# A linear-attention and GELU kernel: one activation table, unit loads of 112 rows, a mask and a copy taken bank by bank, and range checks put later

## The chip, the cores and the metric

The kernel runs on one core of one Trainium2 chip. The metric is the device time of one execution in microseconds. Before the change it was 520.96 us, the median of three runs (520.43 to 521.4).

## The reference

A gated linear attention is followed by a feed-forward block with an exact GELU, all in float32.

```python
# q, k, v, alpha: (4, 8, 768, 48); alpha drawn between 0.8 and 1.0
for t in range(S):
    state = alpha[:, :, t, :, None] * state + np.einsum('bhd,bhe->bhde', k[:, :, t], v[:, :, t])
    y[:, :, t] = np.einsum('bhd,bhde->bhe', q[:, :, t], state)
x = y.transpose(0, 2, 1, 3).reshape(3072, 384)
h = x @ w_in                                   # 384 x 2048
g = 0.5 * h * (1.0 + erf(h * inv_sqrt2))
return g @ w_out                               # 2048 x 384
```

## The kernel before

The 3072 tokens are cut into 12 groups of 256 tokens, and each group into two units of four heads, so there are 24 units, numbered 0 to 23. The text writes u0, u1 and so on. A unit goes through these steps:

- **load** (SP, some of the first on ACT's queue): alpha, k and q of the unit into the tiles `ad`, `kd`, `qd` (L165 for units 0 to 3, L168 for the others), and v into `vn` once a group (L170). There are two sets of these tiles, so the load of unit n overwrites what unit n-4 read.
- **scan, times, back, keys** (DVE): a running product of alpha into `pp` (L254) with its two small helpers into `pe` and `rp` (L255, L256), q times it (L259), a running product from the other end into `rp` (L263), k times that (L268).
- **scores** (PE): q against k (L283), and the transposed k (L291), both into one pair of PSUM banks: in each bank the first half holds scores and the second half transposed keys. `sbank` is that pair, `sfirst` an extra one for u1.
- **kn** (ACT, L301) copies the transposed keys out, **mask** (DVE, L306) multiplies the scores by a causal mask into `ss`. Both read both banks of the pair.
- **inside** (PE): scores against v (L323) and keys against v (L340) into `ybank` or `yfirst`. **chain** (DVE, L358, L360) adds up the states, **outer** (PE, L384) multiplies q by them, **carry** (DVE, L365) keeps the last state.
- **xh, xl** (ACT L435, DVE L439): the result split into a rounded part and its rest, in the tile `x`; the last heads go to `z` and are spread into `x` by six small transfers once a group (`spread`, L448, three on SP and three on ACT's queue in the first groups).
- **check** (ACT, L176): two activations per unit that sum how far alpha lies outside its range, into `junk`. Nothing of the normal path reads it before the end; but the load of unit n waits for the checks of unit n-4.

The feed-forward weights come in 16 pieces of 768 KB (`fetch`, L203, three staging buffers `st`), w_in and w_out in turn. A piece is converted into a high and a low part by four steps: ACT copies its top words (L218), DVE joins them (L222), ACT rounds (L232, `wih` or `woh`), DVE subtracts (L235, `wil` or `wol`). The last step frees the staging buffer. Two pieces make one f of eight. The text writes f0 to f7.

A group's feed-forward is eight times gemm1 (PE, L456, 18 matmuls into `hp`), two GELU activations (ACT, L522 and L523), a subtraction (DVE, L528, `glo`) and gemm2 (PE, L540, 12 matmuls into `acc`). Groups 0 to 3 run so, each f as soon as its weights are there; from group 4 on two groups are taken together (`wide1`, `wide2`, L472 and L490).

The order of each engine's instructions is written out by a planner at the end of the kernel: every step is an `Op` with an engine, a guessed cost, a list of steps that it waits for, and a rank. The planner plays them forward in time and emits them in the order of their planned starts. The engines then run these orders strictly, and wait for each other by semaphores. A guess of a cost sets an order and nothing else.

The lines of the change are `load_data`, `turned_out`, `masked`, `plan_unit` and the loop that plans the units.

Of the kernel before, what the change touches and what calls it, by code (L numbers as in the profile page):

```python
# [16 lines left out]
ALU = mybir.AluOpType  # L17
# [20 lines left out]
def gla_then_gelu_ffn(ctx: ExitStack, tc: tile.TileContext, q, k, v, alpha, qg, kg, ag, vg, q0, k0, a0, w_in, w_out, out):  # L38
# [61 lines left out]
    def small_bank(shape, name):  # L100
        t = sbank
        n = 1
        for d in shape[1:]:
            n *= d
        t = t[:, 0, :n]
        return t if len(shape) == 2 else t.rearrange("p (a b) -> p a b", a=shape[1])

    warm = small_bank([P, P], "warm")
# [50 lines left out]
    def load_data(g, u):  # L159
        n, p = NU * g + u, slice(2 * u, 2 * u + 2)  # L160
        for i, (name, first, src) in enumerate((("a", a0, ag), ("k", k0, kg), ("q", q0, qg))):
            to = data[g % NB][name][:, p].rearrange("p a t -> p (a t)")
            if n < NB * NU:
                eng = nc.scalar if n < NU and (i + u) % 2 else nc.sync
                eng.dma_start(to, first[n])  # L165
                continue
            for h in range(2):
                nc.sync.dma_start(to[h * DP : h * DP + D], src[g - NB, u, h])  # L168
        if u == NU - 1:
            nc.sync.dma_start(vbuf[g % NB][:, :, : HV * D], vg[g])  # L170
# [524 lines left out]
    def op(*args, **kw):  # L695
        ops.append(Op(*args, **kw))
        return ops[-1]
# [4 lines left out]
    def plan_unit(n):  # L702
# [12 lines left out]
        d["load"] = op("SP", "load", lambda: load_data(g, u), [old.get(x) for x in ("outer", "scores", "inside", "c0", "c1")], rank=r - 30, lands=2.0, kb=786 if old == {} else 590)  # L715
        d["load"].cost = 0.9 if n < NU else 1.4 if old == {} else 2.6
# [52 lines left out]
    for n in range(n_units):  # L769
        plan_unit(n)  # L770

# [175 lines left out]
def _laid_out(q, k, v, alpha, moe_w_in, moe_w_out):  # L947
# [14 lines left out]
    def spare(x, value):  # L962
        x = x[:2].reshape(4, 2, D, 512)
        return _np.concatenate((x, _np.full((4, 2, 64 - D, 512), value, x.dtype)), axis=2).reshape(4, P, 512)

    qg, kg, ag = grouped(q), grouped(k), grouped(alpha)
    kg = kg.reshape(-1, H // 4, 2, D, 2, 4, 64).swapaxes(4, 5).reshape(ag.shape)
# [6 lines left out]
        "qg": qg[2:],  # L974
        "kg": kg[2:],
        "ag": ag[2:],
# [3 lines left out]
        "q0": spare(qg, 0.0),  # L980
        "k0": spare(kg, 0.0),
        "a0": spare(ag, 1.0),
# [36 lines left out]
```

## Time and profile before

| what | value |
| --- | --- |
| median of three runs | 520.96 us |
| the profiled execution | 520.84 us |
| its span, first to last instruction | 519.0 us |
| around the span | 1.84 us |
| PE busy (matmuls) | 489.8 us, 94% of the span |
| DVE busy | 251.8 us, 49% |
| ACT busy | 200.4 us, 39% |
| mean granted TensorE clock | 0.972 of 2.4 GHz |

The times in the rows are microseconds from the start of the span. PE is the matmul engine, PEld its weight loads, SPq and ACTq the transfers that SP and ACT issue. In a timeline the first column is the start, the second the length, and a bracket says how long the engine had idled before and what it waited for. On one engine instructions overlap by some tens of ns, so the distance from one start to the next is what an instruction takes from the engine.

### The profile page before, as it was taken

Reading aid. Unit: us, or ns where it says so; the run is one execution under the profiler, and the core shown is the slowest. Engines: PE = TensorE matmul, PEld = TensorE weight load, DVE = VectorE, ACT = ScalarE, POOL = GpSimd, SP = SyncE. Lnnn points to the kernel's source line nnn. Section 1 sums busy time; section 2 is a strip of 40 time slices with the busy share of each in tenths; the row PEclk is TensorE's granted clock in tenths of the full one; section 3 lists DMA queues with packets and bytes.
Section 4 is the critical chain, followed back from the end, with each engine's and each line's share of the span. In section 5 each row is a group of like instructions: output and inputs, shape, how many; then the busy total and the mean of one; then the engine's idle time right before and its main releaser. Section 6 shows DMA issues by size and latency. Waiting matters only on the chain.

```text
span 519.0 us, 12171 instructions
## 1 busy us (share of the span) xinstructions
PE 489.8 (94%) x5190; PEld 418.8 (81%) x5190; DVE 251.8 (49%) x486; ACT 200.4 (39%) x386; POOL 31.3 (6%) x42
## 2 busy tenths in 40 slices
PE   5657999999999999999999999999999999999994
PEld 5556889899998999988888777788777788888883
DVE  4879977998888565121111558521433121211212
ACT  1647757445543342222222543232544222231311
POOL 2000001112211111000000101100000000000000
PEclk9569999999999999999999999999999999999998
DMA  8587757325541421000000332300100000100001
GB/s 317 176 268 230 239 145 231 92 58 159 139 129 43 140 80 46 1 30 1 1 1 1 107 92 56 85 1 0 63 18 3 14 1 0 62 0 1 0 1 67
DMA packets 24542, 40.20 MB, mean 77 GB/s; under 512 B 3872, under 2 KB 11616, under 8 KB 24480
## 3 DMA queue, kind: packets, MB, share of 16 engines
q1 hardware_dynamic: 22736, 34.06, 22.0%
q0 software_dynamic: 880, 3.93, 2.0%
q10 hardware_dynamic: 864, 1.34, 0.8%
q8 instruction: 43, 0.70, 0.6%
q14 instruction: 19, 0.16, 0.1%
HBM read 32.24 MB, written 4.72 MB: 71 GB/s over the span
## 4 chain that ended last, share of the span: by engine, by line
PE 82%; DVE 7%; ACT 4%; DMA 4%; issue 1%; SPq 0%; ACTq 0%; DVEq 0%
PE hw L472 26%; PE accw L490 17%; PE acc L540 10%; PE hp L456 9%; PE ybank L490 8%; DMA st<-in_moe_w_in_dram 2%; PE sbank L283 2%; PE sbank L291 2%; PE sbank L323 1%; PE sbank L384 1%; DMA ad<-in_ag_dram 1%; DVE st L222 1%; DVE pp L254 1%; ACT top L218 1%; PE ybank L323 1%
## 5 line engine op out<-in xcount | busy, mean ns | idle before, releaser
L528 DVE TENSOR_TENSOR glo<-hw,ghi 128x512 fp32r<-128x512 f32 x64 | 44.2, 691 | 172.3 <-ACT hw L523 172.3
L472 PE MATMUL hw<-x,wih 128*128 128x512 f32 x384 | 121.9, 398 | 0.0
L522 ACT ACTIVATE ghi<-hw 128x512 fp32r<-128x512 f32 x64 | 38.3, 598 | 177.7 <-PE hw L472 177.7
L472 PEld LDWEIGHTS hw<-x,wih 128*128 128x128 f32 x384 | 71.0, 188 | 16.1
L456 PE MATMUL hp<-x,wih 128*128 128x256 f32 x384 | 73.5, 291 | 7.6 <-DMA x<-z 7.5
L472 PE MATMUL hw<-x,wil 128*128 128x512 f32 x192 | 75.9, 395 | 0.0
L456 PEld LDWEIGHTS hp<-x,wih 128*128 128x128 f32 x384 | 60.9, 194 | 9.0 <-ACT top L218 7.7
L456 PE MATMUL hp<-x,wil 128*128 128x256 f32 x192 | 54.8, 286 | 0.0
L490 PE MATMUL accw<-ghi,woh 128*128 128x512 f32 x128 | 51.1, 399 | 0.0
L490 PE MATMUL accw<-ghi,wol 128*128 128x512 f32 x128 | 50.2, 393 | 0.0
L540 PE MATMUL acc<-woh,ghi 128*128 128x384 f32 x128 | 44.9, 351 | 0.0
L472 PEld LDWEIGHTS hw<-x,wil 128*128 128x128 f32 x192 | 36.0, 188 | 9.0
L540 PE MATMUL acc<-wol,ghi 128*128 128x384 f32 x128 | 43.0, 336 | 0.0
L490 PE MATMUL accw<-glo,woh 128*128 128x512 f32 x128 | 40.3, 391 | 0.0
L522 ACT ACTIVATE ghi<-hp 128x512 fp32r<-128x512 f32 x32 | 19.1, 598 | 52.3 <-PE hp L456 51.3
L523 ACT ACTIVATE hw<-hw 128x512 f32<-128x512 f32 x64 | 37.9, 592 | 0.0
L456 PEld LDWEIGHTS hp<-x,wil 128*128 128x128 f32 x192 | 37.3, 194 | 0.0
L263 DVE TENSOR_TENSOR_SCAN rp<-ad,rp,top 128x255 f32<-128x255 f32 x48 | 36.8, 809 | 0.1
L259 POOL TENSOR_TENSOR qd<-qd,pp 128x512 f32<-128x512 f32 x18 | 23.5, 1308 | 200.6 <-DMA st<-in_moe_w_in_dram 81.6
L528 DVE TENSOR_TENSOR glo<-hp,ghi 128x512 fp32r<-128x512 f32 x32 | 22.0, 686 | 22.3 <-ACT hp L523 22.1
L254 DVE TENSOR_TENSOR_SCAN pp<-ad,top 128x256 f32<-128x256 f32 x48 | 30.4, 675 | 4.9 <-DMA ad<-in_a_dram 4.9
L306 DVE TENSOR_TENSOR ss<-sbank,mask 128x512 f32<-128x512 f32 x23 | 15.9, 690 | 29.3 <-ACT kn L301 29.1
(105 smaller groups left out, 695.3 us busy)
## 6 DMA issues: line engine op xcount, KB each, us to landing
st<-in_moe_w_in_dram SPq DMA_DIRECT2D x8, 768.0 KB, 5.8
st<-in_moe_w_out_dram SPq DMA_DIRECT2D x8, 768.0 KB, 5.8
vn<-in_vg_dram SPq DMA_DIRECT2D x12, 384.0 KB, 5.1
ad<-in_ag_dram SPq DMA_DIRECT2D x40, 96.0 KB, 3.0
kd<-in_kg_dram SPq DMA_DIRECT2D x40, 96.0 KB, 2.3
qd<-in_qg_dram SPq DMA_DIRECT2D x40, 96.0 KB, 2.7
out_dram<-parts POOLq DMA_DIRECT2D x3, 768.0 KB, 3.6
x<-z SPq DMA_DIRECT2D x63, 32.0 KB, 2.0
```

Of the source, the lines that this page charges most:

```text
L254: nc.vector.tensor_tensor_scan(pp[:, i], at[:, i], top, MID, ALU.mult, ALU.min)
L259: (nc.vector if g < NSB else nc.gpsimd).tensor_tensor(out=qt, in0=qt, in1=pp, op=ALU.mult)
L263: nc.vector.tensor_tensor_scan(rp[:, i, G - 2 :: -1], at[:, i, G - 1 : 0 : -1], top[:, 1:], rp[:, i, G - 1 :], ALU.mult, ALU.min)
L283: nc.tensor.matmul(d["s"][o, h, t], lhsT=d["kt"][r, (2 * j + i) * CS : (2 * j + i + 1) * CS], rhs=d["qt"][r, i, t], start=True, stop=True)
L306: nc.vector.tensor_tensor(out=d["ss"], in0=d["s"][:, :, : 2 * C].rearrange("p h (c t) -> p h c t", t=CS), in1=mask.unsqueeze(1).unsqueeze( ...
L456: nc.tensor.matmul(hp[:, j, :], lhsT=a[:, j, i * P : (i + 1) * P], rhs=x[:, i, :], start=(i == 0 and n == 0), stop=(i == NK - 1 and n == 2),)
L472: nc.tensor.matmul(h, lhsT=a[:, j, i * P : (i + 1) * P], rhs=x[:, i, part], start=(i == 0 and n == 0), stop=(i == NK - 1 and n == 2),)
L490: nc.tensor.matmul(acc[i], lhsT=w[:, j, e], rhs=a, start=(f == 0 and k == 0 and w is wo_hi[f2]), stop=(f == NF - 1 and k == 1),)
L522: nc.scalar.activation(ghi, hp, AF.Gelu)
L523: nc.scalar.activation(hp, hp, AF.Gelu)
L528: nc.vector.tensor_tensor(out=glo, in0=hp, in1=ghi.bitcast(F32), op=ALU.subtract)
L540: nc.tensor.matmul(acc[t], lhsT=a[:, j, t * C : (t + 1) * C], rhs=w[:, j, :], start=(first and j == 0 and k == 0 and w is wo_hi[f]), stop= ...
```

## The change

The kernel is changed in six places:

- `nc.scalar.preload_act_table(AF.Gelu)` stands ahead of everything that ACT does.
- All units are loaded by three transfers. Units 0 to 3 still bring 128 rows; the others bring 112 rows in one transfer instead of twice 48. The host array holds 16 filler rows between the two halves of 48.
- The copy of k of units 0 and 1 is two instructions, the second bank first; their mask is two instructions, the first bank first.
- In the plan, the checks of groups 0 and 1 wait for the first `spread`.
- In the plan, the first step of the first two weight pieces waits for the copies of k of units 0 and 1.
- The planner's guesses for loads and for `spread` are changed.

```diff
-            if n < NB * NU:
-                eng = nc.scalar if n < NU and (i + u) % 2 else nc.sync
-                eng.dma_start(to, first[n])
-                continue
-            for h in range(2):
-                nc.sync.dma_start(to[h * DP : h * DP + D], src[g - NB, u, h])
+            rows = slice(0, P if n < NB * NU else DP + D)
+            eng = nc.scalar if n < NU and (i + u) % 2 else nc.sync
+            eng.dma_start(data[g % NB][name][rows, p].rearrange("p a t -> p (a t)"), src[n, rows])
...
-        nc.scalar.copy(d["kn"], d["s"][:, :, 2 * C : 4 * C])
+        for b in (slice(1, 2), slice(0, 1)) if NU * g + u < NU else (slice(0, 2),):
+            nc.scalar.copy(d["kn"][:, b], d["s"][:, b, 2 * C : 4 * C])
...
-        nc.vector.tensor_tensor(
-            out=d["ss"],
-            in0=d["s"][:, :, : 2 * C].rearrange("p h (c t) -> p h c t", t=CS),
-            in1=mask.unsqueeze(1).unsqueeze(1).to_broadcast([P, 2, NCH, CS]),
-            op=ALU.mult,
-        )
+        for b in (slice(0, 1), slice(1, 2)) if NU * g + u < NU else (slice(0, 2),):
+            nc.vector.tensor_tensor(
+                out=d["ss"][:, b],
+                in0=d["s"][:, b, : 2 * C].rearrange("p h (c t) -> p h c t", t=CS),
+                in1=mask.unsqueeze(1).unsqueeze(1).to_broadcast([P, b.stop - b.start, NCH, CS]),
+                op=ALU.mult,
+            )
...
-        d["load"].cost = 0.9 if n < NU else 1.4 if old == {} else 2.6
+        d["load"].cost = 0.9 if n < NU else 1.4
...
             d["c%d" % side] = op("ACT", "check", lambda side=side: range_check(g, u, side), [d["xh"]], rank=200 + n)
+            if g == 1:
+                for o in (unit[u]["c%d" % side], d["c%d" % side]):
+                    o.deps.append(ready_x[0])
         if u == NU - 1:
             ready_x[g] = op("SP", "spread", lambda: spread(g), [d["xl"]], rank=-100, lands=3.2)
-            if g >= NSB:
-                ready_x[g].cost *= 2
+            ready_x[g].cost *= 2 if g >= NSB else 0.8
...
     for n in range(n_units):
         plan_unit(n)
+    for n in range(NU):
+        wops[n]["u"].deps.append(unit[n]["kn"])
```

What the planner makes of it is seen at three places. In the rows below a transfer is `DMA tile<-array`, and numbers behind names only tell buffers apart.

The first is ACT's queue at the start of the program. `kn` is the copy of k, `top` the first step of a weight piece, `sbank` and `sfirst` the scores of u0 and u1. Before:

```order
L165 DMA kd_111<-in_k_dram 128x512
L165 DMA ad_110<-in_a_dram 128x512
L165 DMA qd_112<-in_q_dram 128x512
L218 ACT_TABLE_LOAD
L218 CAST top_168<-st_182 128x768
L301 COPY kn_0_235<-sbank 128x512
L218 CAST top_169<-st_184 128x768
L301 COPY kn_1_312<-sfirst 128x512
```

And now:

```order
L108 ACT_TABLE_LOAD
L165 DMA kd_112<-in_kg_dram 128x512
L165 DMA ad_111<-in_ag_dram 128x512
L165 DMA qd_113<-in_qg_dram 128x512
L299 COPY kn_0_235<-sbank 128x256 x2
L215 CAST top_169<-st_183 128x768
L299 COPY kn_1_314<-sfirst 128x256 x2
L215 CAST top_170<-st_185 128x768
```

The table load has gone ahead of ACT's transfers, and each copy of k ahead of the weight piece that it stood behind. The table load ahead of the first GELU, further down the queue, is gone.

The second is SP's queue around the first `spread`. `st` are weight pieces, `x<-z` is the spread of group 0, and `ad`, `kd`, `qd` behind it is the load of u4. Before:

```order
L170 DMA vn_113<-in_vg_dram 128x4x192
L203 DMA st_380<-in_moe_w_out_dram 128x2x1536
L168 DMA ad_110<-in_ag_dram 48x512 x2
L168 DMA kd_111<-in_kg_dram 48x512 x2
L168 DMA qd_112<-in_qg_dram 48x512 x2
L448 DMA x_351<-z_382 16x512 x3
L203 DMA st_414<-in_moe_w_in_dram 128x2x1536
L203 DMA st_418<-in_moe_w_out_dram 128x2x1536
```

And now:

```order
L167 DMA vn_114<-in_vg_dram 128x4x192
L200 DMA st_384<-in_moe_w_out_dram 128x2x1536
L447 DMA x_360<-z_386 16x512 x3
L200 DMA st_403<-in_moe_w_in_dram 128x2x1536
L200 DMA st_409<-in_moe_w_out_dram 128x2x1536
L200 DMA st_477<-in_moe_w_in_dram 128x2x1536
L165 DMA ad_111<-in_ag_dram 112x512
L165 DMA kd_112<-in_kg_dram 112x512
L165 DMA qd_113<-in_qg_dram 112x512
```

The load of u4 has gone from ahead of the spread to behind three more weight pieces.

The third is the end of gemm1 of f3 (`hp_3`), on PE and on DVE. `ybank<-qd,state` is outer of u3, `sbank<-qd,kd` and `sbank<-ident,kd` the scores of u4, `acc` gemm2. On PE before:

```order
L456 MATMUL hp_3_720<-x_351,wil_144 128x256
L384 MATMUL ybank<-qd_116,state_0_124 48x64 x4
L384 MATMUL ybank<-qd_116,state_1_125 48x64 x4
L384 MATMUL ybank<-qd_116,state_2_126 48x64 x4
L384 MATMUL ybank<-qd_116,state_3_127 48x64 x4
L540 MATMUL acc_0_0_559<-woh_151,ghi 128x384
```

And on PE now:

```order
L455 MATMUL hp_3_739<-x_360,wil_145 128x256
L383 MATMUL ybank<-qd_117,state_0_125 48x64 x4
L383 MATMUL ybank<-qd_117,state_1_126 48x64 x4
L383 MATMUL ybank<-qd_117,state_2_127 48x64 x4
L383 MATMUL ybank<-qd_117,state_3_128 48x64 x4
L280 MATMUL sbank<-qd_113,kd_112 64x64 x16
L288 MATMUL sbank<-ident,kd_112 128x128 x4
L539 MATMUL acc_0_0_549<-woh_153,ghi 128x384
```

On DVE now, at the same place, `state_1` to `state_4` being the chain of u3 and `kd_112` the keys of u4:

```order
L219 SCALAR_TENSOR_TENSOR st_594<-st_594,top_169 128x768
L232 TENSOR_TENSOR wol_161<-st_588,woh_153 128x768
L256 TENSOR_TENSOR qd_113<-qd_113,pp_0_645 128x512
L232 TENSOR_TENSOR wil_146<-st_594,wih_138 128x768
L359 TENSOR_TENSOR state_1_126<-ybank,state_0_125 128x96
L359 TENSOR_TENSOR state_2_127<-ybank,state_1_126 128x96
L359 TENSOR_TENSOR state_3_128<-ybank,state_2_127 128x96
L359 TENSOR_TENSOR state_4_129<-ybank,state_3_128 128x96
L260 SCALAR_TENSOR_TENSOR rp_0_646<-ad_111,rp_0_646,top 128x255 x2
L265 TENSOR_TENSOR kd_112<-kd_112,rp_0_646 128x2x4x64
```

The scores of u4 now stand directly behind outer of u3, where gemm2 stood, and both wait for DVE steps that stand behind four conversion steps and a product.

## Rows read from the trace of the kernel before

**Rows 1.** The page's span in 40 equal slices of 13 us: busy tenths of PE, and the granted TensorE clock in tenths.

```profile
PE   5657999999999999999999999999999999999994
PEclk9569999999999999999999999999999999999998
```

**Rows 2.** Busy time by stretches: the stretch and its length, busy us of each engine with its instructions, the granted clock, the share of the DMA engines in use, GB/s.

```profile
7.70:12.30 4.60, 1.32 (x37) 0.98 (x36) 3.52 (x8) 1.51 (x2) 0.00 (x0) 1.00 1.04 404
12.40:31.90 19.50, 7.81 (x212) 6.62 (x212) 16.12 (x32) 11.22 (x20) 0.00 (x0) 0.50 0.62 204
31.90:36.10 4.20, 4.14 (x22) 3.94 (x22) 4.06 (x8) 0.93 (x1) 0.00 (x0) 0.50 0.74 254
44.00:57.00 13.00, 10.62 (x184) 9.37 (x182) 12.50 (x27) 9.32 (x14) 0.00 (x0) 1.00 0.61 189
```

**Rows 3.** The longest of PE's waits over the whole span: the line, what it waited for, us in total, times, the longest.

```profile
PE hp L456 <- DMA x<-z: 7.5, 1, 7.5
```

**Rows 4.** Timeline of the start: ACT, DVE and PE around the mask of u0, and the mask and inside of u1.

```profile
9.83 0.66 PE L291 MATMUL sbank<-ident,kd 128*128 128x128 f32 x4
10.65 0.67 DVE L259 TENSOR_TENSOR qd<-qd,pp 128x512 f32<-128x512 f32 x1
10.77 1.28 ACT L218 ACT_TABLE_LOAD   x1 [10.77 <-DMA st<-in_moe_w_in_dram]
12.98 0.57 ACT L301 COPY kn<-sbank 128x512 f32<-128x512 f32 x1
13.66 0.69 DVE L306 TENSOR_TENSOR ss<-sbank,mask 128x512 f32<-128x512 f32 x1 [2.33 <-ACT kn L301]
19.26 0.69 DVE L306 TENSOR_TENSOR ss<-sfirst,mask 128x512 f32<-128x512 f32 x1 [0.82 <-ACT kn L301]
20.01 1.13 PE L323 MATMUL yfirst<-ss,vn 64*64 64x64 f32 x32 [0.58 <-DVE ss L306]
22.37 0.25 DVE L358 COPY state<-yfirst 128x96 f32<-128x96 f32 x1
```

**Rows 5.** Steps on 128x256 values, half the size of a copy or a mask, and the spread: timeline of ACT, DVE, SP's and ACT's queues and PE.

```profile
24.84 0.35 ACT L435 CAST z<-yfirst 128x256 fp32r<-128x256 f32 x1
25.09 0.37 ACT L435 CAST x<-yfirst 128x256 fp32r<-128x256 f32 x1
25.49 0.42 DVE L439 TENSOR_TENSOR z<-yfirst,z 128x256 fp32r<-128x256 f32 x1
25.83 0.42 DVE L439 TENSOR_TENSOR x<-yfirst,x 128x256 fp32r<-128x256 f32 x1
29.49 2.07 SPq L448 DMA_DIRECT2D x<-z  x3
31.96 0.77 PE L456 MATMUL hp<-x,wih 128*128 128x256 f32 x2 [7.51 <-DMA x<-z]
```

**Rows 6.** The chain of work that ended last, in order of time (start, us, what): two of its transfers, and a gemm1 at full clock.

```profile
25.35 4.36 DMA ad<-in_ag_dram
31.61 4.59 DMA st<-in_moe_w_in_dram
...
62.10 2.15 PE hp L456 x18
```

**Rows 7.** ACT's timeline: a range check, and the table load ahead of the first GELU.

```profile
25.35 0.73 ACT L176 ACTIVATE junk<-ad,lo_b 128x512 bf16<-128x512 f32 x1
...
37.30 1.28 ACT L522 ACT_TABLE_LOAD   x1
```

**Rows 8.** DVE's timeline in a full stretch. The distance between starts is what a step takes.

```profile
46.76 0.68 DVE L268 TENSOR_TENSOR kd<-kd,rp 128x512 f32<-128x512 f32 x1
47.36 0.95 DVE L222 SCALAR_TENSOR_TENSOR st<-st,top 128x768 int32<-128x768 int32 x1
48.23 0.68 DVE L439 TENSOR_TENSOR x<-ybank,x 128x512 fp32r<-128x512 f32 x1
48.83 0.25 DVE L365 SCALAR_TENSOR_TENSOR state<-state,pe 128x96 f32<-128x96 f32 x1
48.99 1.27 DVE L254 TENSOR_TENSOR_SCAN pp<-ad,top 128x256 f32<-128x256 f32 x2
...
50.58 0.94 DVE L235 TENSOR_TENSOR wil<-st,wih 128x768 fp32r<-128x768 f32 x1
51.44 0.68 DVE L306 TENSOR_TENSOR ss<-sbank,mask 128x512 f32<-128x512 f32 x1
...
55.27 0.68 DVE L528 TENSOR_TENSOR glo<-hp,ghi 128x512 fp32r<-128x512 f32 x1
55.88 1.12 DVE L360 TENSOR_TENSOR state<-ybank,state 128x96 f32<-128x96 f32 x4
56.91 0.95 DVE L235 TENSOR_TENSOR wil<-st,wih 128x768 fp32r<-128x768 f32 x1
...
60.21 1.38 DVE L263 TENSOR_TENSOR_SCAN rp<-ad,rp,top 128x255 f32<-128x255 f32 x2
61.51 0.93 DVE L235 TENSOR_TENSOR wol<-st,woh 128x768 fp32r<-128x768 f32 x1
```

**Rows 9.** PE's timeline at two points that serve as marks: the start of gemm2 of f3, and outer of u5.

```profile
59.85 0.33 PE L540 MATMUL acc<-woh,ghi 128*128 128x384 f32 x1
79.04 0.67 PE L384 MATMUL ybank<-qd,state 48*48 48x64 f32 x32
```

More of the change, by code (lines that the diff above doesn't have):

```diff
@@ L37, in gla_then_gelu_ffn @@
 @with_exitstack
-def gla_then_gelu_ffn(ctx: ExitStack, tc: tile.TileContext, q, k, v, alpha, qg, kg, ag, vg, q0, k0, a0, w_in, w_out, out):
+def gla_then_gelu_ffn(ctx: ExitStack, tc: tile.TileContext, q, k, v, alpha, qg, kg, ag, vg, w_in, w_out, out):
     nc = tc.nc
@@ L106, in small_bank @@
         return t if len(shape) == 2 else t.rearrange("p (a b) -> p a b", a=shape[1])
+    nc.scalar.preload_act_table(AF.Gelu)
     warm = small_bank([P, P], "warm")
@@ L160, in load_data @@
         n, p = NU * g + u, slice(2 * u, 2 * u + 2)
-        for i, (name, first, src) in enumerate((("a", a0, ag), ("k", k0, kg), ("q", q0, qg))):
-            to = data[g % NB][name][:, p].rearrange("p a t -> p (a t)")
-            if n < NB * NU:
-                eng = nc.scalar if n < NU and (i + u) % 2 else nc.sync
-                eng.dma_start(to, first[n])
-                continue
-            for h in range(2):
-                nc.sync.dma_start(to[h * DP : h * DP + D], src[g - NB, u, h])
+        for i, (name, src) in enumerate((("a", ag), ("k", kg), ("q", qg))):
+            rows = slice(0, P if n < NB * NU else DP + D)
+            eng = nc.scalar if n < NU and (i + u) % 2 else nc.sync
+            eng.dma_start(data[g % NB][name][rows, p].rearrange("p a t -> p (a t)"), src[n, rows])
         if u == NU - 1:
@@ L714, in plan_unit @@
         sp, yp, rp = (next((unit[m] for m in range(n - 1, -1, -1) if of(m) is of(n)), {}) for of in (s_of, y_of, room))
-        d["load"] = op("SP", "load", lambda: load_data(g, u), [old.get(x) for x in ("outer", "scores", "inside", "c0", "c1")], rank=r - 30, lands=2.0, kb=786 if old == {} else 590)
-        d["load"].cost = 0.9 if n < NU else 1.4 if old == {} else 2.6
+        d["load"] = op("SP", "load", lambda: load_data(g, u), [old.get(x) for x in ("outer", "scores", "inside", "c0", "c1")], rank=r - 30, lands=2.0, kb=786 if old == {} else 688)
+        d["load"].cost = 0.9 if n < NU else 1.4
         if u == NU - 1:
@@ L962, in spare @@
     def spare(x, value):
[L963 to L967, printed above, removed]
+        x = grouped(x).reshape(-1, 2, D, 512)
+        return _np.concatenate((x, _np.full((len(x), 2, 64 - D, 512), value, x.dtype)), axis=2).reshape(-1, P, 512)
     w_in = _np.concatenate((main, rest), axis=2).reshape(NK, P, DFF // P, P)
@@ L973, in _laid_out @@
         "alpha": alpha.swapaxes(2, 3),
-        "qg": qg[2:],
-        "kg": kg[2:],
-        "ag": ag[2:],
+        "qg": spare(q, 0.0),
+        "kg": spare(k, 0.0).reshape(-1, P, 2, 4, 64).swapaxes(2, 3).reshape(-1, P, 512),
+        "ag": spare(alpha, 1.0),
         "vg": v.reshape(B, H // 4, 2, 2, S // 256, 4, 64, D)
@@ L979, in _laid_out @@
         .reshape(B * (S // 256), P, 4, H // 2 * D),
-        "q0": spare(qg, 0.0),
-        "k0": spare(kg, 0.0),
-        "a0": spare(ag, 1.0),
         "moe_w_in": w_in.transpose(2, 1, 0, 3),
```

## The prediction

> **What bounds the kernel now.** Read the page's slices first [rows 1]. PE is at nine tenths or more in 35 of 40 slices, and the clock is low in slices 2 and 3 and a little at both ends. So nearly all that can be gained without taking matmuls away lies in the first 60 us, where PE idles and runs at half speed. The stretches say how much [rows 2]: from 7.7 to 12.3 us PE works 1.32 us; from 12.4 to 31.9 it works 7.81 of 19.5 us at 0.50, the 1.2 GHz level; after 4.14 busy us of 4.2 the clock is back at 1.00. From 44 to 57 us PE works 10.62 of 13 us while DVE works 12.50: there DVE is full and PE waits for it. From slice 6 on PE is dense. The end therefore moves by what the start of PE's dense work moves.
>
> The longest single wait is gemm1 of f0 for the spread, 7.5 us [rows 3]. Behind it stands a chain that begins with the mask of u0: PE has finished the transposes at 9.83 + 0.66 = 10.49, but ACT, which is to copy them, waits until 10.77 for a weight piece, loads a table for 1.28 us, does the weight step and copies only at 12.98; DVE idles 2.33 us for that copy, and its mask ends at 13.66 + 0.69 = 14.35 [rows 4]. Further on z and x are ready on DVE at 25.83 + 0.42 = 26.25, but SP issues the spread only at 29.49 [rows 5]: a transfer of u4's load in front takes 4.36 us to land, from 25.35 to 29.71, and the chain of waits goes from its landing to the spread [rows 6].
>
> **The change part by part.**
>
> *Table load and order of ACT.* Now both halves of the copy can run from 10.5 us. Steps of half size take 0.37 us on ACT, 0.25 us apart, and 0.42 us on DVE, 0.34 us apart [rows 5]. The copy ends at 10.5 + 0.25 + 0.37 = 11.15. DVE is free from its product at 10.65 + 0.67 = 11.3 [rows 4], so the mask ends at 11.3 + 0.34 + 0.42 = 12.05, 2.3 us earlier. The weight step that stood in front of the copy takes its place behind it on ACT, where nobody waits for it until the join after the chain of u0. The load of the table at the outset stands ahead of three transfers on ACT's queue. Such issues need not wait for ACT's arithmetic, and even if all three came 1.28 us later, k of u0 is used by DVE only after two scans and two products; I cost it at nothing, bounds -0.4 (alpha of u0 then shares the engines with less) and +0.3.
>
> *Mask and copy in halves.* u0's inside now starts from 12.05, and all that follows on DVE and PE up to u1 moves by the same 2.3 us. In u1 the copy takes 0.62 instead of 0.57 us and the mask 0.76 instead of 0.69, so 0.1 us is given back: inside of u1 moves from 20.01 to 17.8, its chain from 22.37 to 20.15 [rows 4].
> The mask of u0 began 0.1 us after the copy had ended [rows 4]. The halves stay in this order here: the copy takes the second bank first, the mask the first bank, which the copy does last, so the mask still stands behind the whole copy. The Trainium skill, "PSUM — Partial Sum Buffer", Specifications, says that ScalarE and VectorE read PSUM in parallel at full speed unless they meet in a bank; by that rule u1's mask could start up to 0.6 us earlier and the result would be 0.6 us lower; no row here shows it, and I stay with the queue order.
>
> *Range checks and u4's load later.* After its chain at 20.15 (1.03 us) DVE does one low part (0.86), one join (0.87) and a carry (0.16) [rows 8], so z's low part starts at 23.1, its end is 23.5, and x's low part ends at 23.85. SP has only a weight piece in front of the spread, issued when the first low part is done, at 22.1. The spread is issued at 23.5. It landed 2.47 us after its issue before (29.49 to 31.96) [rows 5], which gives 26.0; behind the weight piece, which takes 4.59 us from issue to landing [rows 6], it gives 26.7. I take 26.4: gemm1 of f0 starts 5.6 us earlier.
>
> *Transfers of 112 rows.* A load has 3 issues instead of 6 on SP, and a sixth more bytes. The first of them is u4's. It waits for the second check of u0, which stands on ACT behind the GELU of f0 and the copy of u2 and so is done at about 35 us; with 4.36 us to land [rows 6] it is there at 39.5, and DVE's order, with the sums of the step after next, comes to the scan of u4 at about 43. Nothing on the path, bounds -0.3 and +0.5.
>
> *Second table load.* 1.28 us on ACT at 37.30 [rows 7] falls away, but DVE sets the pace there (next step): nothing of its own.
>
> *What is late next: DVE.* From z's low part to the subtraction of f0 DVE has 9.1 us of steps (two halves at 0.34, two joins, three low parts, a product at 0.60, a scan back at 1.30, a k product at 0.60, a scan with helpers at 1.59 [rows 8]) and some 0.5 us for ACT's rounding, which stands behind three spread issues: 32.7. gemm1 of f0 from 26.4, at half clock twice 2.15 us [rows 6], is done before, at 30.7. Then up to the k product of u4 the new DVE order has 3 glo (0.61), 2 masks (0.60), 5 joins (0.87), 2 q products (0.60), 2 chains (1.03), 5 low parts (0.86), 2 scans back (1.30), x (0.60), carry (0.16), 2 k products (0.60) and a scan (1.59) [rows 8]: 21.1 us, with 0.2 for steps that start on a result and 0.6 for the copy of u3: 54.6. There PE waits for DVE: it has all of u0 to u3, four gemm1 and three gemm2 behind it. Before it was at this point at 59.85 [rows 9]. That is -5.25.
>
> *One more hole.* From 54.6 PE has the scores of u4, a gemm2 and inside of u4. The first part of inside takes 1.13 us at half clock [rows 4], so both parts about 1.1 at full clock; I take the same for the scores, and for gemm2 the 2.15 of a gemm1: 58.9. The chain of u4 stands on DVE behind 4.5 us of steps (glo, carry, z and x, mask, join, scan) and takes 0.8 for its three steps: 59.9. I take +1.0 for it, bounds 0 and +2. From there the same work is dense on both sides up to outer of u5, at 79.04 before [rows 9].
>
> Sum: -5.25 + 1.0 = -4.25 against the profiled execution's 520.84 (span 519.0 and 1.84 around it): 516.6. The median of the runs is 0.12 higher, within its own scatter. DVE has slack again later, so I expect the gain to last to the end.
>
> **The rivals.**
>
> *The clock falls in the new holes.* Around the end of gemm1 of f3 PE waits for chain u3 and then for k of u4: from about 51 to 54.6 us it has 0.6 us to do. Before, the clock fell at 12.3 after 4.6 us with 1.32 busy; but it held from 44 to 57 with 10.62 of 13 busy [rows 2]. If it falls once and comes back after 4.2 us of dense work, 2.1 us are lost: 518.7. For a loss against before it must stay down for more than 8.5 us of dense work, 4.25 us of gain being used up: that is so if it falls already in the gaps near 44 and 47 us and doesn't return until the stretch from 60 us on: some 11 us of work to 60 at half clock less 4.5 us of holes that soak it up, and 2.1 after, +8.6, that is 525. The Trainium skill, "TensorE: Matmul & The Clock Gate", HAM oscillation, speaks for this: gaps between short bursts of matmuls let the clock fall and each burst starts cold; the row from 7.7 to 12.3 agrees, the one from 44 to 57 doesn't show it.
>
> *ACT gives half back.* Six range checks now stand together on ACT ahead of the GELU of f2; at 0.73 [rows 7] they take 4.4 us. If that GELU and the copy of u3 come 2 us later than DVE's order needs them, DVE slips with them: 518.6. If it happens twice, or the spread is held as before, the gain is gone: 520.5. Against it: ACT works 9.32 of 13 us in that stretch [rows 2].
>
> *The clock holds at the start.* Inside of u0 now begins before 12.3 us. If the clock stays at 1.00, the 7.81 busy us at half [rows 2] shrink, of which about 1 us stands ahead of DVE's steps: 515.6.
>
> **How the numbers follow.** The sum: 0.52, with its own range 515.8 to 517.6. Clock holds: 0.13. ACT gives half back: 0.14. Clock falls once: 0.06. Gain gone: 0.07. Clock stays down, slower: 0.08. About 0.2%, 1.04 us, is what a measurement here can tell. Faster: 0.52 + 0.13 + 0.14 + 0.06 = 0.85; same 0.07; slower 0.08. The range runs from 514.4, the clock held and both unknown costs at their lower bounds, to 519.4, which leaves the last two cases out.
>
> **What the profile would show.** Right: mask of u0 at about 11.3 with no idle for ACT, gemm1 of f0 near 26.4, no wait of SP on a load's transfer, DVE above 9 tenths from 26 to 60 us, k product of u4 done near 54.6, one table load. Wrong: gemm1 of f0 after 28, DVE idle for ACT around 45 to 48, a clock of 0.50 after 50 us, or PE idle after 75 us that was not there before.

## The result and the profile after

| kernel | median of its runs, us | ratio to the kernel before, 95% interval |
| --- | --- | --- |
| before | 520.94 (519.82 to 522.06) | |
| after | 523.84 (520.48 to 526.17) | 1.0052 [1.0034, 1.007] |
| after, again in a later job | 522.10 (520.51 to 525.57) | 1.0028 [1.0009, 1.0046] |

The change made the kernel slower by 0.3 to 0.5%; 516.6 was forecast. The profiled execution took 524.7 us, 0.9 above the first median; its span is 522.9. The runs scatter more than before, over 5.7 us instead of 2.2. Medians and ratios in this text leave out single executions far above the rest: 528.22 us in e4, 608.26 in e9, 688.6 in e11, and some of the kernel before in the later jobs.

The start came out close to the forecast. ACT, DVE and PE of the kernel after, beside [rows 4, 5]; start, length, and in brackets the idle time before with what ended it:

```profile
0.94 1.28 ACT L108 ACT_TABLE_LOAD   x1 [0.94 <-PEq L1001]
...
10.68 0.76 DVE L305 TENSOR_TENSOR ss<-sbank,mask 128x256 f32<-128x256 f32 x2
...
22.57 1.88 ACTq L447 DMA_DIRECT2D x<-z  x3
```

PE's longest waits, which answer to [rows 3]: us in total, times, the longest.

```profile
PE hp L455 <- DMA x<-z: 5.4, 1, 5.4
PE ybank L339 <- ACT kn L299: 2.6, 1, 2.6
PE ybank L383 <- DVE state L359: 2.6, 2, 1.6
PE acc L539 <- ACT ghi L521: 2.3, 1, 2.3
PE sbank L280 <- DVE kd L265: 1.8, 2, 1.4
```

The mask of u0 starts at 10.68 instead of 13.66 with no idle time before it, and the wait of gemm1 of f0 shrinks from 7.5 to 5.4 us. Between 40 and 84 us PE's waits add up to 8.9 us; before it was 3.9 us in the same stretch. New are the wait for the copy of u5's keys (`kn`, 2.64 us; before at most 0.4) and the one for the GELU of f2 (`ghi`, 2.28 us); PE waited for a chain and for keys before as well, at other places. The same loss shows when PE's busy time is read by stretches, first of the kernel before, then of the kernel after (stretch, length, busy of PE, PEld, DVE, ACT and POOL with their instructions, granted clock, DMA share, GB/s):

```profile
0.00:39.00 39.00, 22.26 (x353) 20.30 (x354) 27.43 (x53) 16.52 (x25) 2.86 (x17) 0.69 0.74 254
39.00:52.00 13.00, 10.11 (x178) 9.08 (x177) 11.89 (x22) 9.17 (x15) 0.00 (x0) 1.00 0.74 228
52.00:65.00 13.00, 11.95 (x193) 11.15 (x193) 12.79 (x25) 10.39 (x18) 0.00 (x0) 1.00 0.75 239
65.00:78.00 13.00, 12.88 (x237) 11.26 (x236) 10.14 (x20) 7.69 (x14) 0.00 (x0) 1.00 0.54 144
```

```profile
0.00:39.00 39.00, 28.03 (x468) 25.19 (x469) 32.36 (x65) 20.15 (x32) 2.86 (x17) 0.78 0.76 265
39.00:52.00 13.00, 10.58 (x157) 9.77 (x157) 11.01 (x19) 9.01 (x17) 0.00 (x0) 1.00 0.92 244
52.00:65.00 13.00, 9.06 (x175) 8.01 (x175) 9.36 (x22) 7.05 (x12) 0.00 (x0) 0.74 0.69 217
65.00:78.00 13.00, 10.36 (x146) 9.65 (x146) 9.77 (x15) 7.09 (x15) 0.00 (x0) 1.00 0.69 199
...
14.00:31.00 17.00, 9.97 (x158) 8.53 (x152) 15.80 (x33) 9.91 (x16) 0.00 (x0) 0.50 0.73 248
55.00:61.70 6.70, 5.72 (x48) 5.39 (x48) 4.25 (x9) 2.66 (x5) 0.00 (x0) 0.50 0.81 297
78.90:82.20 3.30, 3.30 (x28) 3.08 (x29) 3.23 (x7) 0.56 (x2) 0.00 (x0) 0.50 0.84 250
```

Up to 39 us PE is idle 5.8 us less than before (28.03 - 22.26). From 52 to 78 it is idle 5.4 us more (24.83 - 19.42). Over the whole span its idle time is the same: 519.0 - 489.8 = 29.2 us before, 522.9 - 494.0 = 28.9 after. What made the kernel longer is in the busy time, 4.2 us more. Work at 0.50, the 1.2 GHz level, takes twice its time; it was 7.81 + 4.14 = 11.95 us before [rows 2]. Now it is 9.97 + 5.72 + 3.30 = 18.99: half of the difference, 3.5 us, is the price of the lower clock. So the start's gain was given back as holes, and the clock falling at two of these holes made it a loss. This is bookkeeping on one execution. It does not say that a held clock would give back 3.5 us, since PE would then wait for what comes late.

One of the holes in full: SP's queue, ACT and PE of the kernel after, and one of SP's waits.

```profile
65.41 0.34 SPq L165 DMA_DIRECT2D ad<-in_ag_dram  x1
65.84 0.38 SPq L165 DMA_DIRECT2D kd<-in_kg_dram  x1
66.31 0.38 SPq L165 DMA_DIRECT2D qd<-in_qg_dram  x1
66.74 0.61 SPq L167 DMA_DIRECT2D vn<-in_vg_dram  x1
67.45 0.56 SPq L200 DMA_DIRECT2D st<-in_moe_w_in_dram  x1
...
75.36 1.05 ACT L215 CAST top<-st 128x768 f16<-128x768 bf16 x1 [5.21 <-DMA st<-in_moe_w_in_dram]
76.28 0.88 ACT L229 CAST wih<-st 128x768 fp32r<-128x768 f32 x1
77.07 0.58 ACT L299 COPY kn<-sbank 128x512 f32<-128x512 f32 x1
...
77.70 0.56 PE L339 MATMUL ybank<-vn,kn 64*64 64x48 f32 x24 [2.64 <-ACT kn L299]
81.85 0.81 PE L383 MATMUL ybank<-qd,state 48*48 48x64 f32 x32
...
SPq L165 <- ACT junk L173: 4.0, 1, 4.0
```

Read from below: PE waits 2.64 us for ACT's copy of u5; that copy stands behind two steps of a weight piece (w_in of f6), for which ACT waits 5.21 us; the piece was issued at 67.45 behind the four transfers of u7's load, which itself had been held on SP until 65.41 by a range check, and the piece took 7.8 us to land. At 78.9 the clock is at 0.50. In the kernel before, the same piece stood in front of u7's load on SP:

```profile
65.29 0.52 SPq L203 DMA_DIRECT2D st<-in_moe_w_in_dram  x1
66.32 0.80 SPq L168 DMA_DIRECT2D ad<-in_ag_dram  x2
```

An earlier piece, w_out of f4, held ACT 4.05 us, until 57.51. It was issued at 49.72, when its staging buffer came free, behind the loads of u5 and u6, and took 7.7 us to land (4.9 in e6 below, where u6's load is moved). Rows of the kernel after:

```profile
57.51 1.06 ACT L215 CAST top<-st 128x768 f16<-128x768 bf16 x1 [4.05 <-DMA st<-in_moe_w_out_dram]
...
61.67 0.59 ACT L299 COPY kn<-sbank 128x512 f32<-128x512 f32 x1 [1.09 <-DMA x<-z]
63.86 0.67 PE L383 MATMUL ybank<-qd,state 48*48 48x64 f32 x32 [0.96 <-DVE state L359]
```

### The profile page after: what moved, and what is told of

It is laid out like the page before. It is cut to its first block, busy times and chain, and to the rows that moved or that the text cites. A ratio compares the mean times of both kernels' runs of the same rounds, so it can differ in the third digit from the quotient of the medians.

```text
span 522.9 us, 12096 instructions
## 1 busy us (share of the span) xinstructions
PE 494.0 (94%) x5190; PEld 422.7 (81%) x5190; DVE 252.3 (48%) x488; ACT 200.1 (38%) x387; POOL 31.0 (6%) x42
## 4 chain that ended last, share of the span: by engine, by line
PE 81%; DMA 6%; DVE 5%; ACT 4%; issue 1%; ACTq 0%; SPq 0%; DVEq 0%
PE hw L471 26%; PE accw L489 17%; PE acc L539 10%; PE hp L455 10%; PE ybank L489 8%; DMA st<-in_moe_w_out_dram 4%; PE sbank L280 2%; PE sbank L288 2%; DMA st<-in_moe_w_in_dram 1%; PE sbank L322 1%; ACT top L215 1%; PE sbank L383 1%; PE sbank L339 1%; PE ybank L322 1%; DVE pp L251 1%
## 5 line engine op out<-in xcount | busy, mean ns | idle before, releaser
L455 PE MATMUL hp<-x,wih 128*128 128x256 f32 x384 | 74.6, 294 | 5.4 <-DMA x<-z 5.4
L260 DVE TENSOR_TENSOR_SCAN rp<-ad,rp,top 128x255 f32<-128x255 f32 x48 | 38.4, 841 | 0.2
L299 ACT COPY kn<-sbank 128x512 f32<-128x512 f32 (+1 forms) x24 | 13.5, 569 | 44.6 <-PE sbank L288 41.3
```

Source lines behind the costliest of these rows:

```text
L260: nc.vector.tensor_tensor_scan(rp[:, i, G - 2 :: -1], at[:, i, G - 1 : 0 : -1], top[:, 1:], rp[:, i, G - 1 :], ALU.mult, ALU.min)
L299: nc.scalar.copy(d["kn"][:, b], d["s"][:, b, 2 * C : 4 * C])
L455: nc.tensor.matmul(hp[:, j, :], lhsT=a[:, j, i * P : (i + 1) * P], rhs=x[:, i, :], start=(i == 0 and n == 0), stop=(i == NK - 1 and n == 2),)
```

## The experiments

The theory that these rows suggest is called "transfers": the new order puts unit loads on SP in front of weight pieces, the pieces come late, and whatever stands behind them in ACT's strict order is late with them. Its rivals are "operations" (the table, the halves or the larger transfers themselves cost) and "clock" (the fall at 55 is what counts, whatever made the hole). In the table each ratio is to the kernel before on the same chip in the same job.

| run | median us | ratio, 95% interval |
| --- | --- | --- |
| e1 new operations, old order | 519.46 | 0.9983 [0.9969, 0.9996] |
| e2 old operations, new order | 521.43 | 1.0019 [1.0003, 1.0035] |
| e3 loads of u6 and u7 moved back | 520.38 | 0.9991 [0.9979, 1.0004] |
| e4 holes filled, too long | 522.26 | 1.0035 [1.0014, 1.0055] |
| e5 load of u7 alone moved back | 518.72 | 0.9969 [0.9954, 0.9984] |
| e6 u6 behind the spread, and u7 | 517.79 | 0.9958 [0.9942, 0.9974] |
| e7 as e6, two moves on ACT | 518.31 | 0.9954 [0.9937, 0.9971] |
| e8 range checks not held back | 523.00 | 1.0037 [1.0019, 1.0055] |
| e9 as e6, old operations | 519.06 | 0.9974 [0.9958, 0.9990] |
| e10 as e6, holes filled | 518.16 | 0.9949 [0.9931, 0.9968] |
| e11 after, six transfers a load | 521.21 | 1.0015 [0.9999, 1.0031] |
| e12 before and one line | 519.05 | 0.9971 [0.9955, 0.9986] |
| e13 after, again | 522.10 | 1.0028 [1.0009, 1.0046] |
| e14 load of u6 alone moved back | 522.43 | 1.0026 [1.0011, 1.0041] |
| e15 before and two moves | 520.36 | 0.9992 [0.9977, 1.0007] |
| e16 as e7, holes filled | 517.00 | 0.9936 [0.9916, 0.9955] |

**Order or operations.** e1 undoes the edits of the planner and keeps the rest; e2 does the opposite.

From the kernel after to e1 (the lines that carry the edit; the planner's guess for the size of a load goes back as well):

```diff
-        d["load"].cost = 0.9 if n < NU else 1.4
+        d["load"].cost = 0.9 if n < NU else 1.4 if old == {} else 2.6
...
-            if g == 1:
-                for o in (unit[u]["c%d" % side], d["c%d" % side]):
-                    o.deps.append(ready_x[0])
...
-            ready_x[g].cost *= 2 if g >= NSB else 0.8
+            if g >= NSB:
+                ready_x[g].cost *= 2
...
-    for n in range(NU):
-        wops[n]["u"].deps.append(unit[n]["kn"])
```

From the kernel after to e2, cut in the same way:

```diff
-    nc.scalar.preload_act_table(AF.Gelu)
...
-            rows = slice(0, P if n < NB * NU else DP + D)
-            eng.dma_start(data[g % NB][name][rows, p].rearrange("p a t -> p (a t)"), src[n, rows])
...
+            for h in range(2):
+                nc.sync.dma_start(to[h * DP : h * DP + D], src[n, h * DP : h * DP + D])
...
-        for b in (slice(1, 2), slice(0, 1)) if NU * g + u < NU else (slice(0, 2),):
+        for b in (slice(0, 2),):
...
-        for b in (slice(0, 1), slice(1, 2)) if NU * g + u < NU else (slice(0, 2),):
+        for b in (slice(0, 2),):
```

> Theory 'transfers': the new order lets the loads of u5, u6 and u7 stand on SP in front of weight pieces, the DMA engines are full from 40 to 60 us, and the pieces for f4 to f6 come late (ACT waits 4.05 us for one until 57.51 and 5.21 us for another until 75.36). Rival 'operations': the new operations themselves cost (transfers of 112 rows, the table load ahead of ACT's transfers, the halves). Rival 'clock': two holes of 1.62 and 1.36 us in PE before 56 us let the clock fall to 0.50 from 54.9 to 61.7. This kernel has the new operations in the old order (all edits of the planner undone). Transfers and clock: no loss behind 40 us, and at the start at most the 1.28 us of the table: 519.0 to 521.0. Operations: 523 or more.

> The new order with the old operations: table loaded when first needed, copy and mask in one piece, loads in six transfers of 48 rows. Transfers: the loss stays, and the start gives back about 1.3 us for the table in ACT's way: 523 to 526. Clock: the same if the holes near 52 to 56 are there. Operations: the loss is gone and the start is earlier: 516 to 519.

The old order with the new operations is 0.17% faster than the kernel before, 519.46; the new order with the old operations isn't. So the operations don't make the loss. e2 came out lower than expected, between its two ranges, and with the control (e13) at 522.10, itself under its expected range, it can't be told from the changed kernel. How much of the loss the larger transfers might add is taken up under e11.

**Where the loads stand on SP.** Four runs move steps in the finished order, of SP alone, and e13 is the changed kernel as a control.

`behind(a, b)` takes a step out of the list and puts it right after another. The first line alone is e5, the first two are e3, the first and the third e6, the third alone e14.

```diff
+    behind(unit[7]["load"], wops[12]["get"])
+    behind(unit[6]["load"], wops[11]["get"])
+    behind(unit[6]["load"], ready_x[1])
```

> The changed kernel with two moves on SP alone: u6's load behind the third weight piece that followed it, u7's load behind the one weight piece that followed it. All else in the same order. Transfers: the piece that landed at 57.5 lands 2 to 4 us earlier, the one at 75.36 at about 70.8, so that the copy of u5 no longer holds PE for 2.64 us: 517.0 to 520.5. Clock: the holes at 52 to 56 are ahead of both moves, the clock falls as before: 522 to 524.

> The changed kernel with one move on SP: u7's load with its v behind the weight piece of f6 that it stood in front of. Transfers: that piece lands near 71 instead of 75.36, the copy of u5 no longer holds PE for 2.64 us, the clock no longer falls at 78.8 (3.42 us were worked at half there, so 1.7 us): 4.3 us at most, 519.5 to 521.5. Clock alone: the fall at 55 stays, and if that one is what counts, 522.5 to 524.

> As the run with both loads moved back, but u6's load behind the spread of group 1 instead of right in front of it. There ACT's three issues of the spread took 4.24 us and the copy of u4's keys stood behind them until 61.61. Transfers (the queue of DMA work holds the engine that issues): the issues take about 2 us, the copy is done 2 us earlier, 517.5 to 519.5. Rival, PE's clock or DVE set the pace there: no difference, 520.0 to 520.8.

> The changed kernel itself, as a control beside the next three on one chip. All theories: 522.5 to 525.

> The changed kernel with u6's load behind the spread of group 1, and u7's load left where it is, in front of a weight piece. Transfers: the piece awaited until 57.51 lands near 53.7 and the copy of u4 is done 2 to 3 us earlier, but the hole at the copy of u5 (2.64 us and the clock's fall behind it) stays: 520 to 522. If u7's load is the whole loss: no better than the control.

Moving u7's load behind one weight piece, and nothing else, gave 518.72 us, where the kernel after has 523.84 and 522.10 in its two jobs (0.6 to 0.8% by the ratios): more than was expected, and the whole loss. SP, ACT and PE of e5:

```profile
63.26 0.37 SPq L200 DMA_DIRECT2D st<-in_moe_w_in_dram  x1
63.72 0.42 SPq L165 DMA_DIRECT2D ad<-in_ag_dram  x1
...
69.66 1.09 ACT L215 CAST top<-st 128x768 f16<-128x768 bf16 x1 [1.62 <-DVE st L219]
...
72.25 0.69 PE L322 MATMUL ybank<-ss,vn 64*64 64x64 f32 x32
72.77 0.52 PE L339 MATMUL ybank<-vn,kn 64*64 64x48 f32 x24
75.56 0.67 PE L383 MATMUL ybank<-qd,state 48*48 48x64 f32 x32
```

ACT no longer waits for the piece but for DVE, the two parts of inside of u5 follow each other, and outer of u5 starts at 75.56 (after 81.85, before 79.04 [rows 9]). Of the 6.3 us between after and e5, 2.1 are there at outer of u4 already (63.86 and 61.74), ahead of the moved load. The fairer comparison is the profiled execution of e13, which is the kernel after once more and reaches outer of u4 when e5 does:

```profile
61.81 0.67 PE L383 MATMUL ybank<-qd,state 48*48 48x64 f32 x32 [0.96 <-DVE state L359]
...
77.14 0.89 PE L339 MATMUL ybank<-vn,kn 64*64 64x48 f32 x24 [4.13 <-ACT kn L299]
82.10 0.71 PE L383 MATMUL ybank<-qd,state 48*48 48x64 f32 x32
```

From outer of u4 to outer of u5 it takes 20.3 us, e5 13.8. The time of the piece (w_in of f6) from issue to landing goes the same way. Behind u7's load it is 5.3 us (e11) to 9.5 us (e13), and 7.8 in the kernel after; in front of it, in e3, e5, e6, e7, e9, e10 and e16, it is 4.6 to 5.0. In e13 and e3 the piece is issued at nearly the same time, 65.27 and 65.62, so the later issue is not all of it.

u6's load alone (e14) gains nothing against the control. There the copy of u4's keys comes at 58.89, as early as expected, but outer of u4 only at 63.60: PE worked at half clock from 54.7 to 61.5. The profiled execution of e14, 520.57 us, is one of its four fastest, and the hole at the copy of u5 is 0.2 us in it. So u7's load in front of the piece does not make the hole in every execution. In five profiled executions with that order (e4 with its fillings left aside) the hole is 2.6 us (after, 524.7 us), 4.1 (e13, 524.62), 3.5 (e2, 524.5), 1.0 (e11, 519.85) and 0.2 (e14, 520.57). This may be the scatter of the changed kernel; it is not shown for the executions without a trace.

Together with u7's load it matters where u6's goes. Right in front of the spread (e3) the time is 520.38, worse than behind it (e6, 517.79). In e3 the three spread issues of ACT took 4.24 us and the copy of u4 queued behind them:

```profile
57.33 4.24 ACTq L447 DMA_DIRECT2D x<-z  x3
61.61 0.59 ACT L299 COPY kn<-sbank 128x512 f32<-128x512 f32 x1 [3.28 <-DMA x<-z]
```

Behind the spread (e6) it gives 517.79, which can't be told from e5.

**The clock.** Matmuls of the identity ahead of outer of u3 and of the scores of u4, into a bank that the scores write anew: 14 and 12 in e4, 6 and 5 in e10 and e16 (the two calls are left out here).

```diff
+    def filled(count):
+        for _ in range(count):
+            nc.tensor.matmul(
+                sbank[:, 0, :CS], lhsT=ident, rhs=ident[:, :CS], start=True, stop=True, skip_group_check=True
+            )
```

> The changed kernel with 14 matmuls of 64 columns of the identity ahead of outer of u3 and 12 ahead of the scores of u4, into a bank that the scores write anew: they fill the two holes of PE at 52.3 to 53.96 and 54.6 to 55.98. Clock: the clock stays at 1.00 from 54.9 to 61.7, where PE was busy at half speed, and 2 to 3.4 us are gained: 520 to 522. Transfers: the clock may stay up, but the copy of u4's keys stands on ACT behind a weight piece and the spread until 61.67 whatever PE does, and the end is the same: within 0.6 of the changed kernel.

> As the run with u6's load behind the spread, with 6 matmuls of the identity ahead of outer of u3 and 5 ahead of the scores of u4 (14 and 12 took 3.23 and 2.89 us and made PE late; these should take 1.4 and 1.2, less than the holes of 1.63 and 1.36). Clock: it stays at 1.00 where it fell at 55.6 with 3.41 us of work at half, 1.7 us gained: 515.7 to 516.8. If it falls in a later hole instead, or if the engines behind PE set the pace: 517.3 to 518.5.

In e4 the clock held where it had fallen, but PE was late by its own filling, 3.23 + 2.89 us for 26 matmuls, and the clock fell near 64.7, behind two further holes of 1.00 and 1.15 us and within a third of 0.96 (windows of e4):

```profile
55.00:61.80 6.80, 6.01 (x72) 5.56 (x71) 3.10 (x7) 2.40 (x4) 0.00 (x0) 1.00 0.83 299
64.80:71.40 6.60, 6.01 (x55) 5.87 (x56) 4.89 (x9) 4.86 (x11) 0.00 (x0) 0.50 0.40 119
```

In e10 and e16 the filling fitted, and the clock stayed at 1.00 from 31 us in e10 (first row) and from 32 us in e16 up to 500 us; in e6, without it, it was at 0.50 from 55.7 (second row):

```profile
31.00:500.00 469.00, 464.53 (x4877) 397.31 (x4872) 223.97 (x432) 184.76 (x363) 28.11 (x25) 1.00 0.23 69
```

```profile
55.70:58.90 3.20, 3.20 (x12) 3.20 (x12) 2.82 (x6) 1.81 (x3) 0.00 (x0) 0.50 0.57 174
```

Half of these 3.20 us were to be gained. The medians, 518.16 against 517.79, show no gain; 518.16 lies in the range that was given to engines behind PE setting the pace.

**Order on ACT.** e7 has these moves beside those of e6 (`ahead_of` puts a step right before another), e16 also the filling.

```diff
+    ahead_of(unit[4]["kn"], wops[10]["u"])
+    behind(wops[7]["u"], steps[2]["gelu"])
+    behind(wops[7]["c1"], steps[2]["low"])
```

> As the run with u6's load behind the spread, and two more moves: ACT copies u4's keys ahead of the top words of the piece behind it and of the spread's issues; the GELU of f2 stands ahead of the top words of the piece that ACT waited for until 44.79 (PE waited 2.28 us for that GELU), and on DVE its subtraction ahead of that piece's join. If what stands behind a late transfer in a strict queue is what makes the holes: 514.5 to 517.5. If the pieces themselves pace the work, later steps wait instead: 517.5 to 519.5, as without these moves.

> The changed kernel with u6's load behind the spread, u7's behind the piece, the copy of u4's keys and the GELU of f2 ahead of weight steps on ACT, and 6 and 5 matmuls of the identity in the two holes before 55. Clock: 1.00 from 31 us to the end and 1.7 us better than the same without the filling (518.31): 516 to 517. If the clock's fall there costs nothing because the engines behind PE set the pace: 517.7 to 518.7.

e7 removed PE's wait for the GELU of f2, which was down to 0.84 us in e6, and no difference to e6 can be told. e16 has the lowest median of the study, 517.00, 0.64% under the kernel before, in six executions. That is the upper end of what was expected of a held clock, but its interval overlaps that of e7. What the held clock is worth stays open: by the ratios it is 0.1% in one pair (e10, e6) and 0.2% in the other (e16, e7), neither clear of the intervals.

**The edits one by one.**

From the kernel after to e8:

```diff
-            if g == 1:
-                for o in (unit[u]["c%d" % side], d["c%d" % side]):
-                    o.deps.append(ready_x[0])
```

e9 is e6 with the edit of e2, e11 the kernel after with e2's six transfers alone. From the kernel before to e12 (the first two lines) and to e15 (all three):

```diff
+    for n in range(NU):
+        wops[n]["u"].deps.append(unit[n]["kn"])
+    behind(unit[4]["load"], ready_x[0])
```

> The changed kernel without the one edit that holds the range checks of groups 0 and 1 back until the first spread; the planner then makes another order: u4's load again in front of the first spread, u6's behind it and behind three more pieces, u7's behind two pieces. Transfers: the first spread waits for a load as before the change (some 2 to 3 us given back at the start), but no load stands in front of the late pieces and PE has no holes of over 1 us behind 50: 517.5 to 520.5. If the operations or the other edits make the loss: 522 to 524.

> As the run with u6's load behind the spread and u7's behind the weight piece, but with the old operations: no table load at the outset, copy and mask in one piece, loads in six transfers of 48 rows. If the order alone makes the gain (with ACT's copy ahead of the weight step the table load falls into time in which ACT idles; it stood at 2.35 us in the run of the old operations in the new order): 517.3 to 518.6, the same as with the new ones. If the table at the outset or the halves make the gain that the prediction gave them: 519 to 520.5.

> The changed kernel, its order and its other operations kept, with u4's and the later loads in six transfers of 48 rows instead of three of 112. Transfers: 98 KB less in each load ahead of the pieces and twice the issues on SP. If the larger loads are what made the changed kernel 2.4 us slower than the new order with the old operations: 520.5 to 522. If they cost nothing: 523 to 524.5.

> The kernel before with one line of the change alone: a piece's top words wait for the copy of the unit of the same number, so that ACT copies u0's keys first. SP still has u4's load in front of the first spread, and the loads of u6 and u7 stand behind the weight pieces as before. If the first copy sets the start: the 2.3 us of the mask carry through, 518.2 to 519.2. If the spread behind u4's load sets it: 520 to 521.

> The kernel before, old operations, with two moves alone: ACT copies a unit's keys ahead of the weight step (one line), and on SP u4's load stands behind the first spread instead of in front of it. If the start's 5 us carry through when no later load stands in front of a piece: 515.5 to 517.5. If they are used up later by the pace of the weight pieces, whatever the order: 518.3 to 520, as with the one line alone (519.05).

e8 was a miss for "transfers": its 523.00 lies in the range given to the operations or the other edits. gemm1 of f0 waits 8.1 us for the spread, which stands behind u4's load again, as expected; but with other holes behind it the clock was at 0.50 for 6.31 us of work between 43.3 and 50, and the end is no better than the changed kernel's. The whole order is another one there, so e8 separates no cause. e9, at 519.06, lies at the lower edge of the range in which the operations are worth something; its interval overlaps that of e6, so no cost or gain of the operations is shown in this order. e11, at 521.21, lies in the range in which the larger loads cost something, but it can't be told from the control. e12 came out as expected and is the cheap half of the change: one line gives 0.29%. e15 missed both of its ranges, on the slow side, and shows the other half of the lesson. With u4's load behind the spread, gemm1 of f0 starts at 26.85, but the load then stands in front of a weight piece, and PE is held later (SP, ACT and PE of e15):

```profile
24.91 1.58 SPq L168 DMA_DIRECT2D ad<-in_ag_dram  x2
26.59 0.83 SPq L168 DMA_DIRECT2D kd<-in_kg_dram  x2
27.52 0.83 SPq L168 DMA_DIRECT2D qd<-in_qg_dram  x2
28.45 0.39 SPq L203 DMA_DIRECT2D st<-in_moe_w_in_dram  x1
...
33.90 1.07 ACT L218 CAST top<-st 128x768 f16<-128x768 bf16 x1 [4.00 <-DMA st<-in_moe_w_in_dram]
...
38.74 1.04 PE L323 MATMUL ybank<-ss,vn 64*64 64x64 f32 x32 [3.90 <-DVE ss L306]
```

Its time, 520.36, is that of the kernel before. The execution shown is the fastest of its twelve, 518.65; what the others lose beside this hole is not shown.

## Why the prediction was wrong

**Right: the start.** Mask of u0 forecast at 11.3 to 12.05, measured 10.68 to 11.44; spread at 23.5, measured 22.57; gemm1 of f0 at 26.4, measured 26.67; subtraction of f0 at 32.7, measured 32.01. The table load delayed none of ACT's transfers: it ran from 0.94, and the first was issued at 0.97. But the halves and the early table load had no part in this, in the new order. In e2, which has neither, the table load falls at 2.35 us into time in which ACT idles anyway, the mask starts at 10.65, and PE's wait for the spread is 5.6 us. One line that puts the copy ahead of the weight step does it: with that line alone (e12) the mask starts at 10.88.

That gemm1 came so close is luck. The spread was issued 0.9 us earlier than forecast (DVE's first scan began at 4.28 instead of 4.86, in e2 at 4.27 as well, which the sum doesn't have), and took 4.1 us to land where the sum has 2.9. Two slips in the working carry nothing: the copy's sum gives 11.12 and not 11.15, and the lower end of the range, 514.4, does not come out of its terms (515.6 less 0.4 and 0.3 is 514.9).

The forecast took the halves as serial and gave back 0.1 us for them. In u1 the mask starts at 16.08, when the copy, 15.40 and 0.65 long, has ended. By the rule of the Trainium skill, "PSUM — Partial Sum Buffer", Specifications, the two engines could have read different banks at once. No step here does so, and the trace decides nothing on it.

**Mis-sized: from f0 to the k product of u4.** Forecast done at 54.6, measured 55.23 + 0.69 = 55.92:

```profile
45.87 0.96 DVE L219 SCALAR_TENSOR_TENSOR st<-st,top 128x768 int32<-128x768 int32 x1 [1.32 <-ACT top L215]
...
55.23 0.69 DVE L265 TENSOR_TENSOR kd<-kd,rp 128x512 f32<-128x512 f32 x1
```

Counted from the subtraction of f0 the stretch took 23.9 us instead of 21.9. Most of the difference is 1.32 us in which DVE waited for the top words of a weight piece (w_out of f3), until 45.87. The sum counted DVE's steps and took each piece to be there.

**Mis-sized: "one more hole".** Outer of u4 was forecast at 59.9 and came at 63.86. Of these 4.0 us, 1.3 were there at the k product. The hole itself, 0.96 us, has the size of the +1.0. The rest is the clock: PE worked 5.72 us of this stretch at 0.50 and waited for nothing else in it. The copy of u4's keys was late too, at 61.67: ACT had waited 4.05 us for a weight piece, and then the spread's issues stood in front of the copy. In this execution it held nobody, as PE came to these keys at 62.38; in e4, with the clock held, PE waited 1.15 us for the same copy.

**The step that failed:** "From there the same work is dense on both sides up to outer of u5". It wasn't: PE waited 2.64 us for the copy of u5, and outer of u5 started at 81.85 instead of some 74.8 (79.04 less 4.25). PE idle after 75 us and a clock of 0.50 after 50 us are two of the signs that the prediction itself names for being wrong. Behind it stands an omission one step earlier. Under "Range checks and u4's load later" the prediction followed u4's load alone. The new plan moves the other loads as well: u5's from 32.79 to 40.52, u6's from 58.35 to 43.44, and u7's from behind the weight piece w_in of f6 to in front of it. Each has to be followed past every weight piece that stands behind it on SP. With u7's load behind its piece (e5), outer of u5 comes at 75.56 and the profiled span is 2.7 us shorter than before's, 516.3 against 519.0, of the 4.25 that were forecast; by the medians it is 0.31%, or 1.6 us. From outer of u5 to the end the three take much the same time, 440.0 us before, 441.1 after and 440.7 in e5, so most of the loss stands ahead of that mark. Which edit of the planner set that place is not isolated: without the held checks (e8) u7's load stands behind two pieces, but the whole order is another.

**The rivals.** "The clock falls in the new holes" named the right place, between 51 and 55, with a chance of 0.14 in two parts; it fell twice, came back each time, and cost 5.72/2 + 3.30/2 = 4.5 us, less 1.0 that the start saved. The prediction set the Trainium skill, "TensorE: Matmul & The Clock Gate", HAM oscillation, against the row from 44 to 57. The runs agree with the page in that gaps go with the fall: the clock fell at 55, behind a hole of 1.62 us and within one of 1.36, and with these filled it held (e10, e16). But the held clock alone moved no median that can be told. "ACT gives half back" blamed the range checks; what held ACT was weight pieces, 4.05 and 5.21 us of waiting. A range check did hold u7's load on SP, for 4.0 us. "Clock holds at the start" is undecided: in the profiled run of after it was at 0.50 from 14.0, in e5 and e6 from about 18, with the same order up to there, so this differs from run to run.

**Open.** What the larger transfers cost: against the control and e6, e11 and e9 leave room for some 0.3% either way. What a held clock is worth is open too. The scatter of the changed kernel's runs (mean clock 0.966 to 0.978) was not taken apart; the hole at the copy of u5, which is there in some executions and not in others, is the first thing to look at.

## What to carry to other kernels

When steps are moved earlier on a path, list for every queue what now stands in front of what, up to the end of the phase: a load that nobody waits for is dear in front of a transfer that somebody does. In a strict order the loss appears two engines away, here a copy that had its data and stood behind a step that waited for a late piece. A planner's guess that improves the first 35 us reorders the next 50 as well, so the finished order is worth correcting by one move: one load put back was worth 0.6 to 0.8%. All operations of the change together were worth 0.2% in the old order (e1) and nothing that could be measured in the new one (e2, e9).

## What the runs showed of the hardware

- Issuing is not free here when the transfers are queued: three 32 KB issues on ACT's queue took 1.88 us at the first spread of the changed kernel and 4.24 us right behind a load (e3), and ACT's next arithmetic waited for them.
- SP itself can wait for an older transfer to land before it issues. In e11, with six transfers a load, it is 2.4 us between 40 and 50 us, in the row below. In the changed kernel, with three, SP has no such wait there, but some before 40 us, 1.6 us at the longest.

```profile
SPq L169 <- DMA st<-in_moe_w_in_dram: 2.4, 1, 2.4
```

- PE's idle time and the clock are separate accounts: the same idle time in all, 29.2 and 28.9 us, with 11.95 and 18.99 us of work at half clock.
- A table load on an idle ACT was hidden at both places where these runs have it: at 0.94 or at 2.35 us, each 1.28 us long, with the mask of u0 at 10.68 and 10.65.
